# Attention and two expert layers on one core: more of w_in converted ahead of the first unit, its loads ahead of the second batch's, a third buffer of values, block means from half the rows

## The chip, the cores and the metric

The kernel runs on one core of one Trainium2 chip. The metric is the device time of one execution in microseconds (us). TensorE is called PE, VectorE DVE, ScalarE ACT, GpSimd POOL and SyncE SP. SP issues nearly all DMAs, in the order in which they stand in its queue.

## The reference, cut to what matters

Three layers follow each other: a windowed attention with block summaries, a dense layer with a gated activation, and a routed layer of eight experts.

```python
# attention: batch 2, 8 heads, 768 positions, head size 64; blocks of 32, window 16
k_sum = k.reshape(B, H, nb, block, D).max(axis=3)
v_sum = v.reshape(B, H, nb, block, D).mean(axis=3)
scores_l = scale * q @ k^T, masked to |i - j| < window
scores_s = scale * q @ k_sum^T + log(block)
a = softmax(concat(scores_l, scores_s)); out = a @ concat(v, v_sum)
# dense layer on x [1536, 512]: w_in [512, 2048], w_out [2048, 512], stored as float64
h = x @ w_in;  g = h * clip(h + 3, 0, 6) / 6;  y = g @ w_out
# routed layer: every token to one of 8 experts, 192 tokens each
out[mask_e] = relu(y[mask_e] @ w1[e]) @ w2[e]
```

## The kernel before

**Tiles and units.** The 1536 positions are 12 tiles of 128 (n = 0 to 11; six for each batch), and three tiles make a unit (u = 0 to 3). Attention works in halves (n, h) of four heads each. For a half, `front` (L373) multiplies queries with the window of keys on PE (L383) and reduces the scores on DVE (L391); `soften` exponentiates on ACT (L402) and normalises with DVE (L404, L405) and POOL (L406); `turn` transposes the weights on PE (L414), and ACT copies them to a buffer `at` (L416); `values` multiplies with the values on PE (L429). `emit_x` splits a finished tile into a high part on ACT (L447) and a low part on DVE (L78), the form in which the dense layer takes it. `q_prep` transposes the next tile's queries (L353, L355); `window` copies the next tile's keys (L368).

**The weights of the dense layer.** w_in comes as float64 in 16 slices of 512 KB through four buffers `win64` (`w_in_load`, L247). `w_conv` makes float32 of a slice by three DVE instructions (L272), after which the buffer is loaded with the slice four further on; `w_split` makes a high part on ACT (L289) and a low part on POOL (L290).

**The block means of values.** `vsum_load` brings a batch's values with eight rows to a partition (`vs`). The means come of matmuls with a matrix `zones` (`vsum_mul`, L199). For the first batch all eight rows are multiplied and summed by PE; for the second, `vsum` first adds them on POOL (L191) to one row. `vsum_place` copies the means into each of the buffers `VW` that hold values: into the first on DVE (L203), into the second on ACT (L204).

**Order.** There is no scheduler that moves instructions: each engine runs them in the order in which they are recorded. `drive` records several streams against each other: it takes the next piece of the stream that is least far, by hand-given costs and by the shares of the stretch in which each stream is to run. In the first call the streams are `prologue()` (unit 0's attention, total `ATTS[0]`, and the first half of tile 3) and the conversion of the first `AHEAD` slices, which begins at the share `S0`. In the second call they are the dense layer's first matmul for unit 0 (`gemm1`, L621 to L623: 12 matmuls for each of 16 columns f, results in two PSUM banks in turn), attention of unit 1, and the rest of the conversion. For each f, ACT copies the bank (L624) and DVE gates it (L637), which frees the bank for the f after next. The list `soon` holds work such as loads and low parts that is recorded after the next piece. Keys of the second batch are transposed in `kprep` (L334) ahead of tile 6.

Of the kernel before, what the change touches and what calls it, by code (L numbers as in the profile page):

```python
# [43 lines left out]
SEEK, COUNT = 4600, 1900  # L44
ROUTE = 100000
CLAG = 2
AHEAD = 4
EARLY = 13
LEFT = 4
VLAG = 0  # L50
VN = 3
ATTS = [31212, 20565, 23910, 18810]
END = [0.92, 0.92, 0.92]
S0 = 0.27
S1 = 0.7
LX = 4
TAIL = [0, 1], [2]
# [31 lines left out]
def build(ctx, tc, q, k, v, w_in, w_out, w_gate, w1, w2, out):  # L89
# [54 lines left out]
    LAG = 2  # L144
    Abuf = [att.tile([128, 4, KEYS], FT, name=f"A{i}") for i in range(LAG + 1)]
    kw = att.tile([128, HP, 2, KEYS], FT)
    VW = [att.tile([128, 2, H, D], FT, name=f"VW{i}") for i in range(2)]

    def warm(n):

# [13 lines left out]
    def load_rows(kind, src, b, i):  # L164
        if src is k:
            x = k1[i % 4]
        else:
            x = att.tile([128, H, D], FT, name="raw", bufs=3)
        SP.dma_start(x, src[b, :, i * 128:(i + 1) * 128, :].rearrange("h s d -> s h d"))
        raw[kind, b, i] = x  # L170

# [3 lines left out]
    def load_v(n):  # L175

        b, i = divmod(n, 6)
        for g in range(2):
            lo = i * 128 + g * QG - W
            a, z = max(lo, 0), min(lo + WIN, S)  # L180
            SP.dma_start(VW[n % 2][a - lo:z - lo, g], v[b, :, a:z, :].rearrange("h s d -> s h d"))

    RH = [slice(4 * i, 4 * i + 4) for i in range(2)]

# [3 lines left out]
    def vsum(b):  # L188
        m = KR // 2
        while m:  # L190
            POOL.tensor_tensor(vs[:, :, :m], vs[:, :, :m], vs[:, :, m:2 * m], op=OP.add)  # L191
            m //= 2

    means = []

    def vsum_mul(i, last):
        if i == 0:
            means.append(bank(4))
        PE.matmul(means[-1][:KEYS], zones, vs[:, :, i], start=i == 0, stop=last)  # L199

    def vsum_place():
        pv = means[-1][WIN:KEYS, None].rearrange("p a (h d) -> p a h d", d=D).to_broadcast([NB, 2, H, D])
        DVE.tensor_copy(VW[0][WIN:KEYS], pv)  # L203
        ACT.activation(VW[1][WIN:KEYS], pv, AF.Copy)  # L204

    for g in range(2):
        hs = slice(HP * g, HP * g + HP)
# [202 lines left out]
    def turn(n, h):  # L410
        A = Abuf[(2 * n + h) % (LAG + 1)]
        p = bank(2)
        for c in range(4):
            PE.transpose(p[:KEYS, c * 128:(c + 1) * 128], A[:, c], ident)  # L414
        at = att.tile([128, 4, 128], FT, name="at", bufs=3)
        ACT.activation(at[:KEYS], p[:KEYS].rearrange("p (c s) -> p c s", c=4), AF.Copy)  # L416
        ats[n, h] = at

    def values(n, h):
        vw = VW[n % 2]  # L420
        if h == 0:
            xps[n] = bank(4 if n % 2 else 7)
        at = ats.pop((n, h))
        for pr in range(2):
            hp = 2 * h + pr
            for g in range(2):
                at0 = hp * 128 + g * QG
                for s in range(2):
                    PE.matmul(xps[n][64 * s:64 * s + 64, at0:at0 + QG], vw[:KEYS, g, 2 * hp + s, :],  # L429
                              at[:KEYS, 2 * pr + s, g * QG:(g + 1) * QG], start=True, stop=True, skip_group_check=True)  # L430
        if h == 1:
            u, j = divmod(n, UT)
            xlater.append(n)
            if n + 2 < NT:
                soon.append(partial(load_v, n + 2))

    def emit_x():
        while xlater:
# [14 lines left out]
    def halves():  # L453
        for n in range(UT, NT):
            b, i = divmod(n, 6)
            if b and i == 0:
                vsum(b)
                yield from kprep(b)
                q_prep(n)
                window(n)  # L460
                yield 2400
            for h in range(2):
                t = pend.pop(0) if len(pend) >= LAG else None
                if t:
                    turn(*t)
                    turned.append(t)
                    yield 660
                after = h == 1 and i < 5
                first = (n, h) == (UT, 1)
                if not first:  # L470
                    front(n, h, after)
                    yield 1250 + 450 * after
                pend.append((n, h))
                while turned:
                    if turned[0] == (6 * b, 0):
                        vsum_mul(0, True)
                        vsum_place()
                    values(*turned.pop(0))
                    yield 1000
                emit_x()  # L480
                if first:
                    yield 1
                    front(n, h, after)
                    yield 1250 + 450 * after
                yield from soften()
                emit_x()
                if (n, h) == (UT, 0):
                    for g in range(2):
                        vsum_load(1, g)
                    for j in range(4):  # L490
                        load_rows("kraw", k, 1, j)
            if i == 5:
                while pend or turned:
                    if turned:
                        yield 700
                        values(*turned.pop(0))
                        yield 1000
                        emit_x()
                    if pend:
                        yield 800  # L500
                        t = pend.pop(0)
                        turn(*t)
                        turned.append(t)
                        yield 660
# [269 lines left out]
    def prologue():  # L774
        soft = []

        def half(n, h, after=False):
            front(n, h, after)
            soft.append(soften())
            next(soft[-1])  # L780
            pend.append((n, h))
# [14 lines left out]
        yield 600  # L796
        for c in kprep_first(1):
            yield c
        half(0, 0)
        yield 1250  # L800
        qprep_first(1)
        window(0, slice(2, 4))
        yield 600
        half(0, 1, True)
        rest()
        yield 1250
        def block_means(i):
            for j in range(i, i + 2):
                vsum_mul(j, j == KR - 1)

        def both(t):
            values(*t)
            emit_x()
# [1 line left out]
        half(1, 0)  # L815
        rest()
        yield 1250
        block_means(0)
        yield 1700
        turned_one()  # L820
        yield 660
        block_means(2)
        yield 1700
        half(1, 1, True)
        rest()
        yield 1700
        turned_one()
        yield 660
        block_means(4)
        yield 1700  # L830
        half(2, 0)
        rest()
        yield 1250
        block_means(6)
        vsum_place()
        yield 1700
        turned_one()
        yield 660
        for i in range(2):
            both(turned.pop(0))  # L840
            yield 1000
        half(2, 1, True)
        rest()
        yield 1700
        turned_one()
        yield 660
        both(turned.pop(0))
        yield 1000
        rest()
        yield from attend_unit(0)  # L850

    w_in_load(0)
    for g in range(2):
        vsum_load(0, g)
    w_in_load(1)
    load_v(0)
    load_v(1)
    for j in range(2, NW):
        w_in_load(j)
    for n in range(2):  # L860
        load_rows("qraw", q, 0, UT + n)

    def splits():
        for s in range(NF + CLAG):
# [439 lines left out]
```

## Time and profile before

| | us |
|---|---|
| median of 3 runs (587.82 to 588.29) | 587.87 |
| the profiled execution | 584.98 |
| its span | 583.0 |
| PE busy | 548.8 |
| DVE busy | 356.2 |
| ACT busy | 291.7 |
| POOL busy | 163.9 |

The page gives busy time by engine and groups of instructions by source line and shape; the views used below are cut from the same trace. A time in brackets behind a row is how long the engine stood idle before it, and what is taken to have ended that idleness. PEclk is the clock that PE was granted, as a share of 2.4 GHz. A busy time of PE includes the overlap of matmuls that follow each other.

### The profile page before, as it was taken

What the parts mean: (1) busy time and instruction counts of PE and PEld (TensorE: products, weight loads), DVE (VectorE), ACT (ScalarE), POOL (GpSimd) and SP (SyncE); (2) the same over time, 40 slices, a digit from 0 to 9 for tenths busy, and PEclk for the clock granted to TensorE, in tenths of its full rate; (3) what the DMA queues carried; (4) which work ended last, traced back from release to release, by engine and by line L of the source; (5) the groups of instructions that cost most, each with busy time, mean ns of one, the idle gap of its engine ahead of it and who ended that gap; (6) DMA issues with size and microseconds to landing.
All of it is one profiled execution on the core that took longest, in us unless ns stands there. A gap on an engine that the chain in (4) does not pass through costs nothing.

```text
span 583.0 us, 10815 instructions
## 1 busy us (share of the span) xinstructions
PE 548.8 (94%) x3867; PEld 458.5 (79%) x3867; DVE 356.2 (61%) x1022; ACT 291.7 (50%) x698; POOL 163.9 (28%) x197
## 2 busy tenths in 40 slices
PE   6768789989999999999999999999999999999993
PEld 6447678879889989986677777778789888988882
DVE  6577795644543288750045655553588888888880
ACT  4556464456544445561132232234576777677750
POOL 1124348111111032582244444456001100111011
PEclk9789899999999999999999999999999999999998
DMA  9978962302110145430042000004589888998811
GB/s 235 231 193 171 276 177 48 77 20 47 28 36 19 47 141 176 140 105 2 1 126 91 1 1 1 1 18 183 155 262 289 251 242 249 288 254 233 255 47 33
DMA packets 98270, 75.05 MB, mean 129 GB/s; under 512 B 38112, under 2 KB 84704, under 8 KB 98208
## 3 DMA queue, kind: packets, MB, share of 16 engines
q1 hardware_dynamic: 96224, 67.96, 43.2%
q0 software_dynamic: 1984, 6.32, 3.0%
q8 instruction: 33, 0.54, 0.4%
q14 instruction: 29, 0.24, 0.1%
HBM read 67.55 MB, written 6.71 MB: 127 GB/s over the span
## 4 chain that ended last, share of the span: by engine, by line
PE 53%; issue 27%; DVE 8%; DMA 5%; POOL 3%; ACT 2%; SPq 0%; POOLq 0%; DVEq 0%; ACTq 0%
PE bank L738 8%; PE bank L739 7%; PE bank L740 7%; PE bank L621 6%; PE bank L622 5%; PE bank L623 5%; POOL out_dram L1107 3%; DVE bank L272 2%; PE bank L649 2%; PE bank L383 2%; PE bank L199 2%; PE bank L429 2%; PE bank L414 1%; DMA big<-in_moe_w_out_dram 1%; PE bank L309 1%
## 5 line engine op out<-in xcount | busy, mean ns | idle before, releaser
L621 PE MATMUL bank<-x,wh 128*128 128x384 f32 x256 | 91.7, 358 | 4.2 <-DVE t L637 2.1
L299 DVE TENSOR_TENSOR wl<-t,wh 128x1024 fp32r<-128x1024 f32 x64 | 77.0, 1220 | 20.5 <-ACT wh L298 18.1
L623 PE MATMUL bank<-x,wl 128*128 128x384 f32 x256 | 86.7, 339 | 2.5 <-POOL wl L290 2.5
L622 PE MATMUL bank<-x,wh 128*128 128x384 f32 x256 | 86.4, 338 | 0.4 <-DVE x L78 0.3
L715 ACT ACTIVATE thx<-t 128x384 fp32r<-128x384 f32 (+2 forms) x80 | 36.2, 459 | 94.6 <-PE bank L739 94.0
L624 ACT ACTIVATE t<-bank,three 128x384 f32<-128x384 f32 x64 | 37.1, 580 | 89.1 <-PE bank L623 87.1
L738 PE MATMUL bank<-wh,thx 128*128 128x512 f32 x192 | 79.2, 412 | 0.0
L716 POOL TENSOR_TENSOR tlx<-t,thx 128x384 fp32r<-128x384 f32 (+1 forms) x56 | 56.0, 1002 | 77.4 <-ACT thx L715 70.7
L740 PE MATMUL bank<-wh,tlx 128*128 128x512 f32 x192 | 75.3, 392 | 0.1
L739 PE MATMUL bank<-wl,thx 128*128 128x512 f32 x192 | 75.0, 390 | 0.0
L1132 PE MATMUL bank<-x,wh 128*128 128x384 f32 x256 | 73.7, 360 | 0.5 <-DVE x L1058 0.5
L298 ACT ACTIVATE wh<-t 128x1024 fp32r<-128x1024 f32 x64 | 65.6, 1047 | 0.0
L1134 PE MATMUL bank<-x,wl 128*128 128x192 f32 x256 | 64.2, 251 | 0.0
L637 DVE SCALAR_TENSOR_TENSOR t<-t,bank 128x384 f32<-128x384 f32 x64 | 34.9, 549 | 41.1 <-ACT t L624 41.1
L406 POOL TENSOR_TENSOR A<-A,sm 128x480 f32<-128x480 f32 x24 | 23.7, 987 | 128.0 <-ACT at L416 65.8
L1107 POOL DMA_INDIRECT out_dram<-t,idx x16 | 14.9, 931 | 141.5 <-DVE t L1156 136.0
L621 PEld LDWEIGHTS bank<-x,wh 128*128 128x128 f32 x256 | 48.2, 188 | 8.3 <-DVE t L637 3.1
L623 PEld LDWEIGHTS bank<-x,wl 128*128 128x128 f32 x256 | 48.3, 189 | 3.2 <-POOL wl L290 3.2
L622 PEld LDWEIGHTS bank<-x,wh 128*128 128x128 f32 x256 | 48.5, 189 | 1.0 <-DVE x L78 0.9
L1134 PEld LDWEIGHTS bank<-x,wl 128*128 128x128 f32 x256 | 48.9, 191 | 0.3
L1132 PEld LDWEIGHTS bank<-x,wh 128*128 128x128 f32 x256 | 48.1, 188 | 1.2 <-DVE x L1058 0.8
L1148 PE MATMUL bank<-wh,t 128*128 128x512 f32 x128 | 48.9, 391 | 0.0
(194 smaller groups left out, 1014.5 us busy)
## 6 DMA issues: line engine op xcount, KB each, us to landing
t<-in_moe_w_dram SPq DMA_DIRECT2D x128, 256.0 KB, 4.5
t<-in_moe_w_in_dram SPq DMA_DIRECT2D x16, 512.0 KB, 5.7
big<-in_moe_w_out_dram SPq DMA_DIRECT2D x16, 512.0 KB, 3.3
VW<-in_v_dram SPq DMA_DIRECT2D x20, 192.0 KB, 3.7
t<-in_v_dram SPq DMA_DIRECT2D x4, 768.0 KB, 11.8
raw<-in_q_dram SPq DMA_DIRECT2D x9, 256.0 KB, 4.7
t<-xs SPq DMA_DIRECT2D x8, 258.0 KB, 4.4
t<-in_k_dram SPq DMA_DIRECT2D x4, 384.0 KB, 6.0
```

Of the source, the lines that this page charges most:

```text
L298: ACT.activation(hi, x, AF.Copy)
L299: DVE.tensor_tensor(lo, x, hi.bitcast(FT), op=OP.subtract)
L621: PE.matmul(p, wh[:, kk, :], xh[:, kk, :], start=kk == 0, stop=False)
L622: PE.matmul(p, wh[:, kk, :], xl[:, kk, :], start=False, stop=False)
L623: PE.matmul(p, wl[:, kk, :], xh[:, kk, :], start=False, stop=kk == KD - 1)
L716: (DVE if placed[0] else POOL).tensor_tensor(ths[i][1], t, ths[i][0].bitcast(FT), op=OP.subtract)
L738: PE.matmul(acc[j], th[:, c], WH[s], start=f == 0, stop=False)
L739: PE.matmul(acc[j], th[:, c], WL[s], start=False, stop=False)
L740: PE.matmul(acc[j], tl[:, c], WH[s], start=False, stop=f == NF - 1)
L1132: PE.matmul(p, a[:, kk, :], xt[:, kk].rearrange("p c s -> p (c s)"), start=kk == 0, stop=False, skip_group_check=True)
L1134: PE.matmul(p[:, :CAP], b[:, kk, :], xt[:, kk, 0, :], start=False, stop=kk == KD - 1, skip_group_check=True)
L1148: PE.matmul(p, x, w, start=m == 0 and i == 0, stop=m == NM - 1 and i == 2)
```

## The change

Six slices of w_in instead of four are converted in the first call of `drive`, whose total and starting share are changed with it (`AHEAD`, `ATTS[0]`, `S0`). There are three buffers of values instead of two, and the load of tile n + 3 instead of n + 2 follows the values of tile n. Buffers `raw` (queries) and `at` go from three to two. For the first batch, DVE adds the upper four rows of `vs` to the lower four, and PE multiplies four rows instead of eight. The first loads stand in another order, and the second batch's loads of keys and values are recorded in tile 5 instead of tile 3, keys first. In the prologue, the second part of the query preparation stands between the scores and the softmax of the first half, and some pieces stand in another order.

```diff
-AHEAD = 4
+AHEAD = 6
-ATTS = [31212, 20565, 23910, 18810]
+ATTS = [27812, 20565, 23910, 18810]
-S0 = 0.27
+S0 = 0.3
...
-    VW = [att.tile([128, 2, H, D], FT, name=f"VW{i}") for i in range(2)]
+    VW = [att.tile([128, 2, H, D], FT, name=f"VW{i}") for i in range(3)]
...
-            x = att.tile([128, H, D], FT, name="raw", bufs=3)
+            x = att.tile([128, H, D], FT, name="raw", bufs=2)
...
     def vsum(b):
         m = KR // 2
         while m:
-            POOL.tensor_tensor(vs[:, :, :m], vs[:, :, :m], vs[:, :, m:2 * m], op=OP.add)
-            m //= 2
+            (POOL if b else DVE).tensor_tensor(vs[:, :, :m], vs[:, :, :m], vs[:, :, m:2 * m], op=OP.add)
+            m = m // 2 if b else 0
...
-        ACT.activation(VW[1][WIN:KEYS], pv, AF.Copy)
+        for x in VW[1:]:
+            ACT.activation(x[WIN:KEYS], pv, AF.Copy)
...
-        at = att.tile([128, 4, 128], FT, name="at", bufs=3)
+        at = att.tile([128, 4, 128], FT, name="at", bufs=2)
...
-            if n + 2 < NT:
-                soon.append(partial(load_v, n + 2))
+            if n + 3 < NT:
+                soon.append(partial(load_v, n + 3))
...
-                if (n, h) == (UT, 0):
+                if (n, h) == (5, 0):
+                    for j in range(4):
+                        load_rows("kraw", k, 1, j)
                     for g in range(2):
                         vsum_load(1, g)
-                    for j in range(4):
-                        load_rows("kraw", k, 1, j)
...
-        half(0, 0)
-        yield 1250
+        front(0, 0, False)
         qprep_first(1)
+        soft.append(soften())
+        next(soft[-1])
+        pend.append((0, 0))
+        yield 1850
         window(0, slice(2, 4))
-        yield 600
         half(0, 1, True)
...
-                vsum_mul(j, j == KR - 1)
+                vsum_mul(j, j == KR // 2 - 1)
...
         half(1, 0)
         rest()
         yield 1250
-        block_means(0)
-        yield 1700
+        vsum(0)
         turned_one()
...
     for g in range(2):
         vsum_load(0, g)
+    load_v(0)
     w_in_load(1)
-    load_v(0)
+    w_in_load(2)
     load_v(1)
-    for j in range(2, NW):
-        w_in_load(j)
-    for n in range(2):
-        load_rows("qraw", q, 0, UT + n)
+    w_in_load(3)
+    load_rows("qraw", q, 0, UT)
+    load_v(2)
+    load_rows("qraw", q, 0, UT + 1)
```

Lines of the changed kernel below the new ones are numbered one to three higher.

SP's queue around the second batch's loads, before (in_moe_w_in_dram is w_in; VW_94 and VW_95 are the buffers of values, raw is a tile of queries, t<-in_v_dram the values for the block means):

```order
L247 DMA t<-in_moe_w_in_dram 128x4x256 x2
L181 DMA VW_94<-in_v_dram 96x8x64 x2
L169 DMA raw<-in_q_dram 128x8x64
L247 DMA t<-in_moe_w_in_dram 128x4x256
L181 DMA VW_95<-in_v_dram 96x8x64 x2
L173 DMA t<-in_v_dram 96x8x256 x2
L169 DMA t<-in_k_dram 128x8x64 x4
L247 DMA t<-in_moe_w_in_dram 128x4x256
L181 DMA VW_94<-in_v_dram 96x8x64 x2
```

SP's queue around the same loads now:

```order
L248 DMA t<-in_moe_w_in_dram 128x4x256 x3
L169 DMA raw<-in_q_dram 128x8x64
L248 DMA t<-in_moe_w_in_dram 128x4x256
L181 DMA VW_94<-in_v_dram 80x8x64
L181 DMA VW_94<-in_v_dram 96x8x64
L248 DMA t<-in_moe_w_in_dram 128x4x256 x2
L169 DMA t<-in_k_dram 128x8x64 x4
L173 DMA t<-in_v_dram 96x8x256 x2
L181 DMA VW_95<-in_v_dram 96x8x64 x2
```

The batch's loads stood ahead of nine slices of w_in, the first of them right behind; now the last two of w_in stand right ahead of them.

DVE in the prologue, between the scores of half (1, 0) and those of half (1, 1), before (bank_337 is scratch of the conversion):

```order
L404 TENSOR_SCALAR sm<-sm 128x4
L405 RECIPROCAL sm<-sm 128x4
L272 TENSOR_SCALAR bank_337<-t 128x512
L272 SCALAR_TENSOR_TENSOR bank_337<-t,bank_337 128x512
L272 SCALAR_TENSOR_TENSOR t<-t,bank_337 128x512
L391 ISA A_90,sm<-bank_353,mask 128x120
```

DVE at the same place now, with the addition of values (L191) among the conversion:

```order
L405 TENSOR_SCALAR sm<-sm 128x4
L406 RECIPROCAL sm<-sm 128x4
L273 TENSOR_SCALAR bank_341<-t 128x512
L191 TENSOR_TENSOR t<-t 96x8x256
L273 SCALAR_TENSOR_TENSOR bank_341<-t,bank_341 128x512
L392 ISA A_90,sm<-bank_352,mask 128x120
```

The addition came in, and the last step of the conversion moved behind the scores of (1, 1).

## Rows read from the trace of the kernel before

**Rows 1.** Busy time by engine in long stretches; (x) counts instructions:

```profile
core 0: us, PE busy (x) PEld busy (x) DVE busy (x) ACT busy (x) POOL busy (x), PEclk, DMA share, GB/s
0.00:50.00 50.00, 35.45 (x448) 25.92 (x449) 31.58 (x128) 26.29 (x82) 11.51 (x19) 0.86 0.87 206
50.00:93.50 43.50, 37.66 (x315) 32.90 (x313) 38.49 (x105) 25.04 (x73) 20.96 (x19) 0.96 0.87 201
93.50:250.00 156.50, 152.29 (x1231) 138.47 (x1231) 85.75 (x258) 79.76 (x213) 39.95 (x35) 1.00 0.26 72
250.00:583.00 333.00, 323.36 (x1880) 261.20 (x1877) 200.39 (x534) 160.56 (x331) 91.47 (x127) 0.99 0.45 134
```

**Rows 2.** The same view, finer, with the same columns:

```profile
25.30:39.00 13.70, 9.52 (x103) 5.15 (x103) 10.29 (x42) 6.43 (x21) 2.62 (x3) 1.00 0.87 232
39.00:45.80 6.80, 5.94 (x66) 4.81 (x67) 2.36 (x13) 3.72 (x13) 2.54 (x3) 0.50 0.34 92
45.80:50.00 4.20, 2.67 (x56) 2.13 (x53) 2.38 (x6) 3.68 (x12) 1.54 (x2) 1.00 0.78 168
64.30:93.50 29.20, 23.45 (x195) 20.07 (x193) 28.09 (x72) 16.02 (x46) 15.44 (x14) 0.94 0.74 190
69.70:73.10 3.40, 3.40 (x24) 2.96 (x26) 3.26 (x5) 1.25 (x3) 0.74 (x2) 0.50 1.09 310
```

**Rows 3.** Timeline of PE's weight loads: start, us, instruction, [idle before, releaser]:

```profile
66.30 0.19 PEld L621 LDWEIGHTS bank<-x,wh 128*128 128x128 f32 x1 [1.10 <-ACT wh L289]
68.91 0.19 PEld L623 LDWEIGHTS bank<-x,wl 128*128 128x128 f32 x1 [2.31 <-POOL wl L290]
...
93.51 0.19 PEld L621 LDWEIGHTS bank<-x,wh 128*128 128x128 f32 x1 [1.06 <-DVE t L637]
```

**Rows 4.** Timeline of SP's queue and DVE; then loads, with KB, us to landing:

```profile
47.75 10.88 SPq L169 DMA_DIRECT2D t<-in_k_dram  x4
58.72 1.17 SPq L247 DMA_DIRECT2D t<-in_moe_w_in_dram  x1
64.31 0.69 DVE L272 TENSOR_SCALAR bank<-t 128x512 int32<-128x512 int32 x1 [3.21 <-DMA t<-in_moe_w_in_dram]
...
t<-in_v_dram SPq DMA_DIRECT2D x2, 768.0 KB, 9.2
```

**Rows 5.** Stretch, DVE busy (count), clock, DMA share, GB/s of line L272 alone:

```profile
50.00:93.50 43.50, 24.20 (x36) 0.96 0.87 201
```

**Rows 6.** Timeline of PE and DVE in the prologue:

```profile
16.99 0.95 PE L383 MATMUL bank<-kw,t 64*64 64x120 f32 x16 [1.80 <-ACT t L324]
27.89 0.28 DVE L391 CUSTOM_DVE_ANT_0 A<-bank,mask 128x120 f32<-128x120 f32 x1 [3.38 <-PE bank L383]
38.86 0.97 PE L353 MATMUL bank<-ident,raw 128*128 128x128 f32 x4 [2.86 <-issue]
...
43.60 1.08 PE L383 MATMUL bank<-kw,qT 64*64 64x120 f32 x16
49.03 0.64 PE L383 MATMUL bank<-kw,qT 64*64 64x120 f32 x16
50.01 0.42 PE L621 MATMUL bank<-x,wh 128*128 128x384 f32 x1
```

**Rows 7.** Groups by line, 0 to 50 us; L299 of the whole span: busy, mean ns:

```profile
L199 PE MATMUL bank<-t,zones 96*120 96x512 f32 x16 | 9.6, 729 | 0.0
L204 ACT ACTIVATE VW<-bank 24x1024 f32<-24x1024 f32 x1 | 1.0, 1017 | 1.1 <-DVE VW L203 1.1
L213 POOL MEMSET VW<- 128x1024 f32 x2 | 1.8, 941 | 0.0
...
L299 DVE TENSOR_TENSOR wl<-t,wh 128x1024 fp32r<-128x1024 f32 x64 | 77.0, 1220 | 20.5 <-ACT wh L298 18.1 <-DMA t<-in_moe_w_dram 2.4
```

**Rows 8.** Timeline around the second batch's start, POOL and PE:

```profile
96.05 8.43 POOL L191 TENSOR_TENSOR t<-t 96x2048 f32<-96x2048 f32 x3
101.17 0.60 PE L334 MATMUL bank<-ident,t 128*128 128x128 f32 x4
119.75 0.99 POOL L406 TENSOR_TENSOR A<-A,sm 128x480 f32<-128x480 f32 x1 [15.27 <-ACT qT L355]
```

More of the change, by code (lines that the diff above doesn't have):

```diff
@@ L180, in load_v @@
             a, z = max(lo, 0), min(lo + WIN, S)
-            SP.dma_start(VW[n % 2][a - lo:z - lo, g], v[b, :, a:z, :].rearrange("h s d -> s h d"))
+            SP.dma_start(VW[n % 3][a - lo:z - lo, g], v[b, :, a:z, :].rearrange("h s d -> s h d"))
     RH = [slice(4 * i, 4 * i + 4) for i in range(2)]
@@ L419, in values @@
     def values(n, h):
-        vw = VW[n % 2]
+        vw = VW[n % 3]
         if h == 0:
@@ L817, in prologue @@
         yield 1250
-        block_means(0)
-        yield 1700
+        vsum(0)
         turned_one()
         yield 660
-        block_means(2)
-        yield 1700
         half(1, 1, True)
@@ L828, in prologue @@
         yield 660
-        block_means(4)
+        block_means(0)
         yield 1700
@@ L833, in prologue @@
         yield 1250
-        block_means(6)
+        block_means(2)
         vsum_place()
         yield 1700
[L837 to L844, printed above, removed]
+        both(turned.pop(0))
+        yield 1000
         turned_one()
@@ L848, in prologue @@
         yield 1000
+        half(2, 1, True)
+        rest()
+        yield 1700
+        both(turned.pop(0))
+        yield 1000
+        turned_one()
+        yield 660
         rest()
```

## The prediction

> **What bounds the kernel now.** I read the stretches of the trace first [rows 1]. Behind 93.5 us TensorE (PE) is busy 152.29 of 156.5 us and then 323.36 of 333 us: the change touches nothing that costs time there, and PE sets it. The losses lie ahead: in the prologue (0 to 50 us) the granted clock is 0.86 and no engine is full, and in the first 43.5 us of unit 0 PE is busy 37.66 us, but VectorE (DVE) 38.49 us. Next come the finer stretches [rows 2]: from 64.3 to 93.5 us DVE is busy 28.09 of 29.2 us. There DVE is the bound and PE waits for it. Third, the waits of PE's weight loads between 64 and 94 us [rows 3]: six of over 0.5 us, the first at 66.30 (1.10 us), the last at 93.51 (1.06 us, for the gate of DVE), the longest 2.31 us for the low half of a slice of w_in, and all six together 7.1 us. From 69.7 to 73.1 us PE also runs at a granted clock of 0.50, so it does about 1.7 us less work there.
>
> Fourth, what starts the full stretch of DVE: at 64.31 DVE had stood 3.21 us, waiting for a slice of w_in [rows 4]. That slice's load was issued only at 58.72, because the four loads of the second batch's keys had occupied the issue queue of SP for 10.88 us from 47.75. These loads are wanted only at 101.17 us, when PE transposes the keys [rows 8].
>
> **The change, part by part.**
>
> *Unit 0.* Six slices instead of four are converted before its first matmul. The 36 DVE instructions of L272 from 50 to 93.5 us take 24.20 us [rows 5], 0.67 us each; two slices are six of them, 4.0 us. The 3.2 us wait goes too: the SP order puts keys and block-mean loads of batch two behind the last slice of w_in, and the slices that unit 0 wants then wait only for a free buffer, which an earlier conversion frees well ahead (counted from zero, slice seven's buffer comes free when slice three is converted, before unit 0 starts). So DVE needs 38.5 - 4.0 = 34.5 us plus the 43.5 - 38.5 - 3.2 = 1.8 us in which it stood otherwise: 36.3 us. PE alone needs 43.5 - 7.1 - 1.7 = 34.7 us. DVE stays the bound, but by only 1.6 us, so now and then the two will wait for each other in turn: I take 37.3 us, with 36.2 and 38.0 as ends of this case. Gain 6.2 us. Late next is DVE's gate again, and behind the last slice PE.
>
> *Start of unit 0.* Three things move it; before it starts at 50.01 [rows 6]. (a) Query preparation is put ahead of the first softmax: ACT copies the queries before eight softmax instructions instead of after them. The second score matmuls, which stood 1.80 us for that copy and began at 16.99, can begin about 0.9 us earlier, when the key windows are there. (b) The means: eight matmuls (16 rows) cost 9.6 us [rows 7]; four remain, so 4.8 us of PE go. A DVE addition over 96 x 2048 elements comes instead. An addition of 1024 elements takes 1.22 us [rows 7], so this takes between 1.2 us (that row itself) and 2.45 us (twice it); it has twice the elements, so I take 2.4. It cannot start before both halves of the values have landed and stands in DVE's order ahead of the next score reduction. By hand, that reduction moves from 27.89 [rows 6] to about 25.5: PE's scores are ready near 22.9, and the addition eats half of what the absent matmuls give. (c) Two more slices, 4.0 us, go between DVE's reductions, most behind the second and third query tile. From 25.5 I walk DVE's new order: window copies and a normalisation 2.8 us, four conversions 2.7, the reduction of (2,0) at 30.4; copy of the means at 31.6 to 32.9, when values can start on PE. ACT now copies the means twice, 1.02 us each [rows 7], so the third tile copy and, behind it, the first output come about a microsecond later than the copy of the means alone would ask: the query transposes that began at 38.86 [rows 6] begin at 37.5. From there ACT is the chain (softmax, tile copy, tile copy, softmax, output), as before, and reaches the first matmul of unit 0 at 48.6, a lead of 1.4 us.
>
> That walk has all matmuls at the full clock. The trace grants 0.50 from 39.0 to 45.8 [rows 2], after PE was busy 9.52 of 13.7 us with holes. At half clock scores take 1.08 us instead of 0.64 [rows 6]. The new order has less PE work in this stretch, so I expect the low level at least as long. About eight bursts of 0.4 us more come, half of them behind an ACT that is late anyway: 1.6 us. Ends: 1.4 us earlier and 1.0 us later (all eight on the path and a slow first 1 us of unit 0); I take 0.2 us earlier.
>
> The Trainium skill speaks against this part of the change: "TensorE: Matmul & The Clock Gate", section "What's actually happening", says that the throttled clock is the default and activity releases it, so taking matmuls out of a thin stretch can cost clock. The trace agrees so far that low stretches follow thin ones. By that rule the start would be the late end, and the sum 1.2 us worse.
>
> *At no cost.* The third memset of a value buffer (0.94 us [rows 7]) lies on POOL while PE waits for the first keys; constants behind it reach DVE about 0.9 us later, against a first use that stands at least as long behind PE. Two tile buffers and two query buffers instead of three: each tile copy now waits for the values two tiles before it, which PE has already done in either order; a query load waits for transposes two tiles before, and SP's queue holds slices of w_in behind it, which are not wanted for some 10 us. If that cover went, it would cost DVE the 3.2 us again.
>
> *Second batch.* Its loads go out when slice eleven frees its buffer, by the walk near 72 us, where they were issued at 47.75 [rows 4]. The four loads of keys, 10.88 us of issue, are in by about 84 us, and the values, which took 9.2 us to land [rows 4], by about 93. PE wants the keys at 101.17 less 6.4, near 95. POOL's addition of values takes 8.43 us [rows 8]: it began at 96.05 and would now run from 93 to 101.5, ahead of a normalisation that came at 119.75 after 15.27 us of idleness and now comes near 113. Cover is some 11 us for each. No cost.
>
> **Sum.** The profiled execution took 584.98 us, its span 583.0; the median of the other runs is 587.87, 2.9 us more. Against the profile: 584.98 - 6.2 - 0.2 = 578.6. The parts move a stretch by the same microseconds in either kind of run, so against the median: 587.87 - 6.4 = **581.5 us**. The ends of this case: 36.2 with the early start gives 579.2, 38.0 with the late start 583.4.
>
> **Rivals.** (1) *The prologue is DVE's.* If the 6.4 us that DVE gains there (4.0 + 2.4) all lie on the path and only the 4.8 us of matmuls leave it, unit 0 starts 1.6 us late, and 1 to 3 us of low clock come on top; with 6.2 us gained later that gives 583.4 to 586.7. For it: each reduction now stands behind conversions. Against: DVE is busy only 31.58 of the first 50 us [rows 1], and ACT is the chain at the end. (2) *PE becomes the bound of unit 0*: 34.7 us, and the start 1.4 us early: 587.87 - 8.8 - 1.4 = 577.7. For it: DVE's margin is 1.6 us. Against: the two engines wait for each other through two banks. (3) *The clock, and slower than before.* If PE stays at the low level from 25.3 us into unit 0, some 5.5 us of matmuls (9.52 less the means) and the 2.67 us of [rows 2] double, and the first 7 us of unit 0 lose 3.4: 11.6 us, against a gain of 7.6 without it, gives 591.9. It decides from 7.6 us of added matmul time on the path. Against: clock came back at 45.8 although the stretch ahead of it had only two thirds of its time filled. (4) *It doesn't do what it says*: the slices' loads still come late, since a load needs its buffer and SP waits in order behind query loads that now wait for a buffer; DVE still stands 3.2 us, and what it is spared in unit 0 (4.0 us) it pays in the prologue: 586.7 to 589. Against: buffers come free before 48 us by the walk.
>
> **Chances.** Forecast 0.53, rival 1 0.20, rival 2 0.13, rival 3 0.06, rival 4 0.08. A measurement of this kernel can tell about 0.2% (1.2 us) from no change. Faster 0.53 + 0.20 + 0.13 = 0.86, same 0.08, slower 0.06. The range 578.0 to 586.7 leaves out rivals 3 and 4 and the lower half of rival 2, 0.2 together.
>
> **What would show it.** In the new profile the first matmul of unit 0 starts between 48.6 and 51 us; DVE has no wait of over 1 us for w_in there; PE's waits for DVE and POOL in unit 0 fall from 7.1 to 2 or 3 us; the step that ended at 93.5 ends near 87; the stretches behind it keep their lengths to 1 us; keys land before PE asks for them. Wrong would be: a start behind 52 us, granted clock 0.50 inside unit 0 for more than 3.4 us, DVE waiting for the values ahead of the addition, or PE waiting for the second batch's keys.

## The result, and the profile after

The changed kernel takes 582.81 us (median of 4 runs, 581.76 to 583.78) where the kernel before takes 587.85 us beside it (4 runs, 587.59 to 588.29). The ratio is 0.9913, with an interval of 0.9894 to 0.9933: 5.0 us faster, between 3.9 and 6.2 us. The prediction said 6.4 us. Its sum has two terms, and the trace of after shows them apart: the gain in unit 0 came nearly as worked out, and the start of unit 0, forecast 0.2 us earlier, came 2.4 us later.

The stretches of after, cut where those of [rows 1] are cut (first matmul of unit 0; the wait of PE for DVE's gate that stands last in [rows 3]; the end of unit 3). The columns are start:end, length, busy time of PE, PE's weight loads, DVE, ACT and POOL (instructions in brackets), granted clock, share and rate of DMA:

```profile
0.00:52.40 52.40, 39.64 (x440) 28.64 (x441) 40.07 (x138) 28.11 (x85) 15.68 (x22) 0.69 0.96 218
52.40:90.10 37.70, 36.00 (x315) 32.31 (x313) 33.73 (x96) 24.31 (x72) 17.94 (x16) 0.98 0.87 194
90.10:246.60 156.50, 152.40 (x1231) 138.56 (x1232) 85.36 (x257) 80.34 (x214) 39.92 (x35) 1.00 0.27 74
246.60:580.00 333.40, 323.50 (x1879) 260.98 (x1877) 200.88 (x534) 160.61 (x331) 91.45 (x127) 0.99 0.45 134
...
19.50:53.70 34.20, 28.36 (x224) 18.23 (x221) 27.23 (x89) 17.88 (x57) 11.86 (x11) 0.50 0.95 208
```

The second row took 43.5 us before and takes 37.7. The third is as long as before to 0.1 us and the fourth to 0.4. The first is 2.4 us longer, with a clock of 0.69 where it had 0.86. The last row says why: from 19.5 to 53.7 us PE was at a granted clock of 0.50, the lower of its two levels, without a break, 1.2 us of it inside unit 0. Before, the same level stood from 18.5 to 25.3 and from 39.0 to 45.8.

A finer ruler for unit 0 is the first output of its first and of its thirteenth column, the ACT instruction that reads PE's result. First before, then after (start, us, instruction, [idle before, releaser]):

```profile
52.75 0.58 ACT L624 ACTIVATE t<-bank,three 128x384 f32<-128x384 f32 x1 [1.80 <-DMA t<-in_v_dram]
95.92 0.58 ACT L624 ACTIVATE t<-bank,three 128x384 f32<-128x384 f32 x1 [0.73 <-PE bank L623]
```

```profile
55.39 0.58 ACT L625 ACTIVATE t<-bank,three 128x384 f32<-128x384 f32 x1 [1.96 <-PE bank L624]
92.50 0.58 ACT L625 ACTIVATE t<-bank,three 128x384 f32<-128x384 f32 x1 [1.80 <-PE bank L624]
```

From first to thirteenth is 43.17 us before and 37.11 after: 6.06 us less. The experiments below are read by this distance. (The lines of after lie one lower: L272 is now L273.)

What DVE waited for from 50 to 95 us in after (us in total, times, longest), and its conversions in unit 0 alone (busy, count):

```profile
DVE t L638 <- ACT t L625: 4.3, 4, 1.8
DVE sm L405 <- ACT A L403: 1.0, 1, 1.0
DVE x L78 <- ACT x L448: 0.7, 1, 0.7
```

```profile
52.40:90.10 37.70, 20.60 (x30) 0.98 0.87 194
```

No wait for a slice of w_in is left, against the 3.21 us of [rows 4], and 30 instructions of 20.60 us stand where 36 of 24.20 us stood [rows 5]. What DVE waits for now is ACT, which waits for PE. PE's weight loads still wait in four places, where [rows 3] sums six to 7.1 us:

```profile
71.39 0.19 PEld L622 LDWEIGHTS bank<-x,wh 128*128 128x128 f32 x1 [0.34 <-DVE t L638]
73.94 0.55 PEld L430 LDWEIGHTS bank<-at,VW 120*64 120x64 f32 x16 [0.50 <-ACT at L417]
...
78.12 0.19 PEld L622 LDWEIGHTS bank<-x,wh 128*128 128x128 f32 x1 [0.99 <-DVE t L638]
...
90.08 0.19 PEld L622 LDWEIGHTS bank<-x,wh 128*128 128x128 f32 x1 [0.81 <-DVE t L638]
```

That is 2.6 us, three of the four for DVE's gate. But PE is now the fuller of the two, 36.00 against DVE's 33.73 of 37.70 us, and the chain of work that ended last changes sides (start, us, engine and line; each row is the last or the first of its stretch):

```profile
67.19 0.19 PE bank L624
67.44 0.15 DVE A L392
...
78.12 0.44 PE bank L622
...
83.39 0.58 ACT t L625
...
90.08 0.45 PE bank L622
```

It lies on PE up to 67.4 and from 78.1 to 83.4, some 21 us in all, on DVE for some 14 us, and on ACT and POOL for most of the rest. Neither engine alone bounds unit 0 any more.

The prologue is read in the chain of work that ended last (start, us, engine and line):

```profile
22.22 2.70 DVE t L191
24.95 3.77 PE bank L199 x4
28.72 1.01 PE bank L384 x16
29.73 3.71 PE bank L199 x4
33.47 1.24 DVE VW L203
...
39.40 1.13 PE bank L354 x4
...
43.80 1.08 PE bank L415 x4
44.88 1.01 PE bank L384 x16
...
51.75 1.04 PE bank L354 x4
```

The addition (L191) and both pairs of mean matmuls (L199) lie on it. Eight rows of the means take 7.5 us at the low clock, where sixteen took 9.6 us before [rows 7]. Halving them has brought PE 2.1 us, not 4.8. Each burst of scores or transposes behind them takes 1.0 to 1.1 us, where [rows 6] has 0.64 at the full clock.

The second batch, on SP, POOL and PE, for [rows 4, 8]:

```profile
77.25 4.30 SPq L169 DMA_DIRECT2D t<-in_k_dram  x4
81.59 2.00 SPq L173 DMA_DIRECT2D t<-in_v_dram  x2
```

```profile
93.66 8.45 POOL L191 TENSOR_TENSOR t<-t 96x2048 f32<-96x2048 f32 x3 [1.18 <-PE bank L415]
...
116.32 0.99 POOL L407 TENSOR_TENSOR A<-A,sm 128x480 f32<-128x480 f32 x1 [14.22 <-ACT qT L356]
```

```profile
97.75 0.60 PE L335 MATMUL bank<-ident,t 128*128 128x128 f32 x4
```

The keys' loads, issued 29.5 us later than before, take 4.30 us of SP instead of 10.88, and PE's first transposes of them (97.75) wait for nothing. POOL's addition starts at 93.66, where the prediction had 93, and the next normalisation behind it had stood 14.22 us for something else. That this move costs nothing was right.

One thing does not fit to the microsecond. The two profiled executions are 3.2 us apart (584.98 and 581.76 us), the medians 5.0. The profiled execution of before was 2.9 us under its median, that of after 1.1 us. The start of unit 0 moves between executions: the kernel with only the loads moved, whose prologue is that of before, started it at 50.72, not 50.01, and the run with two value buffers, whose prologue is that of after but for a memset, a copy of the means and a load, at 51.39, not 52.45. So the start is a term of some 1 to 2.4 us, and single traces don't settle it closer.

### The profile page after: what moved, and what is told of

Read it like the earlier page. It is cut to its first block, busy times and chain, and to the rows that moved or that the text cites. A ratio compares the mean times of both kernels' runs of the same rounds, so it can differ in the third digit from the quotient of the medians.

```text
span 580.0 us, 10816 instructions
## 1 busy us (share of the span) xinstructions
PE 551.5 (95%) x3859; PEld 460.5 (79%) x3859; DVE 360.0 (62%) x1023; ACT 293.4 (51%) x700; POOL 165.0 (28%) x198
## 4 chain that ended last, share of the span: by engine, by line
PE 54%; issue 27%; DVE 6%; POOL 5%; DMA 3%; ACT 3%; SPq 0%; POOLq 0%; DVEq 0%; ACTq 0%
PE bank L739 7%; PE bank L622 7%; PE bank L741 6%; PE bank L740 6%; PE bank L624 6%; PE bank L623 6%; POOL out_dram L1110 3%; PE bank L430 2%; POOL xs L672 2%; PE bank L384 2%; PE bank L650 2%; ACT A L403 2%; PE bank L199 1%; PE bank L415 1%; PE bank L310 1%
## 5 line engine op out<-in xcount | busy, mean ns | idle before, releaser
L299 ACT ACTIVATE wh<-t 128x1024 fp32r<-128x1024 f32 x64 | 65.6, 1048 | 0.0
L1137 PEld LDWEIGHTS bank<-x,wl 128*128 128x128 f32 x256 | 48.9, 191 | 0.3
L1151 PE MATMUL bank<-wh,t 128*128 128x512 f32 x128 | 48.9, 391 | 0.0
```

The costliest lines, as they stand in the source:

```text
L299: ACT.activation(hi, x, AF.Copy)
L1137: PE.matmul(p[:, :CAP], b[:, kk, :], xt[:, kk, 0, :], start=False, stop=kk == KD - 1, skip_group_check=True)
L1151: PE.matmul(p, x, w, start=m == 0 and i == 0, stop=m == NM - 1 and i == 2)
```

## Experiments

All ratios are against the kernel before, run beside each kernel. *Lead* is the time from the first score matmul to the first matmul of unit 0 (this leaves out how early the scores could start, which moves by 1.7 us between executions), *unit 0* the distance from the first to the thirteenth column as above, *low clock* the stretches at 0.50 between 15 and 95 us. The last three columns come from the one profiled execution of each kernel.

| kernel | median | ratio, interval | lead | unit 0 | low clock |
|---|---|---|---|---|---|
| before | | | 36.92 | 43.17 | 18.5–25.3, 39.0–45.8, 69.7–73.1 |
| after | 582.81 | 0.9913, 0.9894–0.9933 | 38.89 | 37.11 | 19.5–53.7 |
| means8 | 581.48 | 0.9914, 0.9886–0.9943 | 36.92 | 37.10 | 21.2–28.1, 45.1–52.0 |
| warm | 580.77 | 0.9906, 0.9873–0.9940 | 36.26 | 37.10 | none |
| loads_back | 586.80 | 0.9990, 0.9961–1.0018 | 37.65 | 42.02 | 21.6–48.9, 72.8–79.6 |
| ahead4 | 584.11 | 0.9938, 0.9908–0.9969 | 38.60 | 40.29 | 18.9–53.1 |
| loads_only | 584.16 | 0.9960, 0.9935–0.9985 | 36.91 | 40.32 | 19.7–26.5, 40.2–47.0 |
| ahead_only | 582.29 | 0.9910, 0.9874–0.9945 | 37.66 | 37.24 | 20.2–27.1, 37.3–47.5 |
| values2 | 582.33 | 0.9923, 0.9896–0.9950 | 37.66 | 37.11 | 20.1–47.4 |
| ahead_loads | 582.10 | 0.9914, 0.9892–0.9935 | 37.94 | 37.10 | 21.7–28.5, 38.8–49.0 |
| means8_warm | 579.21 | 0.9859, 0.9832–0.9886 | 36.70 | 37.10 | 38.3–41.7 |
| ahead_warm | 580.86 | 0.9886, 0.9863–0.9909 | 38.71 | 37.11 | 37.4–44.2 |

The theory was that unit 0 gains what DVE is spared there, and that the start is late because of the clock. The rival was that the prologue is DVE's: the addition and the two further conversions lie on its path.

### The eight mean matmuls back

```diff
-            for j in range(i, i + 2):
-                vsum_mul(j, j == KR // 2 - 1)
+            for j in range(2 * i, 2 * i + 4):
+                vsum_mul(j, j == KR - 1)
...
-        vsum(0)
```

> The changed kernel, but the first batch's block means come of all eight rows again: no DVE addition (2.77 us in the trace of the changed kernel), eight matmuls instead of four, four at each of the two places. Theory A (the start of unit 0 came late, at 52.45 us, because PE ran at a granted clock of 0.50 from 19.5 to 53.7 us, and it fell and stayed low since the matmuls of the means left): with them back the clock is at 1.00 for at least part of 25 to 50 us, unit 0 starts between 50.5 and 52.5, and the time is 581.5 to 583.5. Rival B (the matmuls themselves are on the path, whatever the clock): four more at 0.9 us each put the start 2 to 4 us later, 585 to 587.

The ratio is that of after, 0.9914 against 0.9913. Its lead, and the score reduction that stands behind the addition in after (at 25.42 there), as windows of all engines (columns as in the first fence) and as a row of DVE:

```profile
14.52:51.44 36.92, 27.25 (x298) 17.61 (x297) 27.89 (x111) 22.06 (x75) 11.90 (x11) 0.82 1.10 224
```

```profile
23.82 0.27 DVE L392 CUSTOM_DVE_ANT_0 A<-bank,mask 128x120 f32<-128x120 f32 x1
```

The lead is 1.97 us shorter than in after, the reduction comes 1.6 us earlier, and the granted clock, back at 1.00 from 28.1, stayed there up to 45.1. The four kernels with halved means and no extra matmuls (after, loads_back, ahead4, values2) have the low clock for 27.3 to 34.2 us without a break; this one has it twice for 6.9 us. So halving the means, worth 4.8 us of PE in the prediction, bought nothing here that the times can tell: in the trace, what it saves on PE it gives back as an addition on DVE and as clock. This run alone does not tell the clock from DVE's work, since it changes both.

### After, with the clock held up

Sixty extra matmuls of the identity into a bank that nobody reads, in nine places (three are shown), by the kernel's own helper `warm`; nothing else is touched. The trace counts each as two instructions.

```diff
         qprep_first(1)
+        warm(5)
...
         half(0, 1, True)
+        warm(8)
...
         half(1, 0)
+        warm(5)
```

> The changed kernel with 60 extra matmuls of the identity (128 x 128, float32) into a bank that nobody reads, in the holes of PE between 15 and 46 us; nothing else is changed, the outputs are the same. Theory A (the clock sets the late start of unit 0): the granted clock stays at 1.00 for most of 20 to 50 us, unit 0 starts at 49 to 50.5 instead of 52.45, and the time is 580 to 581.5. Rival B (the conversions and the addition on DVE set the start): the clock rises, but unit 0 still starts at 52 or later, 582.5 to 584.

The lead row of this kernel, and that of after (columns as above):

```profile
14.79:51.05 36.26, 32.14 (x411) 26.62 (x409) 29.67 (x107) 22.30 (x75) 11.30 (x11) 1.00 1.01 218
```

```profile
13.56:52.45 38.89, 30.67 (x291) 19.75 (x289) 30.77 (x112) 22.07 (x75) 11.95 (x11) 0.58 0.96 211
```

With 120 more instructions on PE and nearly the same work on DVE (29.67 against 30.77 us) the lead is 2.63 us shorter. That is the clock, and it speaks against the rival: DVE's addition and conversions are all still there. The start itself, 51.05, lies between the two expectations, because the first scores came late (14.79 against 13.56). The other kernels with this prologue fall in line: 38.89 and 38.60 us of lead with 34.2 us of low clock, 37.65 and 37.66 with 27.3, 36.26 with none. The prediction's walk at the full clock put unit 0's start 35.5 us behind the first scores (48.6 less 13.09); 36.26 came out. The gain is shown in the traces only: the median falls by 2.0 us, but the ratio to the runs beside it by 0.0007, or 0.4 us, and its interval contains that of after.

### The second batch's loads back, and six conversions ahead kept

```diff
-                if (n, h) == (5, 0):
-                    for j in range(4):
-                        load_rows("kraw", k, 1, j)
+                if (n, h) == (UT, 0):
                     for g in range(2):
                         vsum_load(1, g)
+                    for j in range(4):
+                        load_rows("kraw", k, 1, j)
```

> The changed kernel, but the second batch's loads of values and keys are recorded in tile 3 again, as before, ahead of most of w_in's slices. Theory A (3.2 of the 6.2 us that unit 0 gained are the DVE's wait for a slice of w_in): DVE stands 2 to 4 us for w_in in unit 0 again, and the time is 585 to 586.5. Rival C (two slices more in hand cover the queue's delay): no such wait, 582.3 to 583.3.

0.9990: with this one part undone, nothing is left that the times can tell. DVE and SP of this kernel:

```profile
71.87 0.70 DVE L273 TENSOR_SCALAR bank<-t 128x512 int32<-128x512 int32 x1 [5.95 <-DMA t<-in_moe_w_in_dram]
```

```profile
52.85 10.75 SPq L169 DMA_DIRECT2D t<-in_k_dram  x4
63.69 1.68 SPq L181 DMA_DIRECT2D VW<-in_v_dram  x2
65.47 1.10 SPq L248 DMA_DIRECT2D t<-in_moe_w_in_dram  x1
```

The slice behind the keys in SP's queue is issued at 65.47, and DVE, ready for it at 65.92, stands 5.95 us, more than the 2 to 4 us expected. Before, DVE was ready at 61.10 for a slice issued at 58.72: here the keys went out 5.1 us later, and DVE came to its slice only 4.8 us later, 0.45 us behind the issue instead of 2.4.

### Four conversions ahead, with the rest of the change

```diff
-AHEAD = 6
+AHEAD = 4
```

> The changed kernel with four slices converted ahead of unit 0 instead of six. Theory A (DVE bounds unit 0 and 4.0 us of its work were moved ahead into its holes): unit 0's stretch from the first to the thirteenth column grows from 37.1 us by 2.5 to 4, while its start gains at most 1 us; the time is 584.5 to 586. Rival D (with the loads out of the way DVE is no bound any more): the stretch keeps its length to 1 us, 582 to 583.

0.9938, and unit 0 takes 40.29 us (54.94 to 95.23):

```profile
54.94 0.58 ACT L625 ACTIVATE t<-bank,three 128x384 f32<-128x384 f32 x1 [1.84 <-PE bank L624]
95.23 0.58 ACT L625 ACTIVATE t<-bank,three 128x384 f32<-128x384 f32 x1 [0.73 <-PE bank L624]
```

So the six DVE instructions are worth 40.29 - 37.11 = 3.2 us there, where the prediction's term was 4.0. The run also bears on the late start. Its lead row (columns as above):

```profile
13.51:52.11 38.60, 31.16 (x290) 20.10 (x289) 26.45 (x106) 21.25 (x73) 9.35 (x9) 0.57 0.94 202
```

DVE has 4.3 us less to do in the lead than in after (26.45 against 30.77), the clock is as low (0.57 against 0.58), and the lead is only 0.3 us shorter. With the extra matmuls it was the other way round: DVE as busy, the clock up, 2.6 us gained. So by these traces it is the clock that makes the start late, and not the conversions on DVE.

### The loads moved, alone

```diff
-                if (n, h) == (UT, 0):
-                    for g in range(2):
-                        vsum_load(1, g)
+                if (n, h) == (5, 0):
                     for j in range(4):
                         load_rows("kraw", k, 1, j)
+                    for g in range(2):
+                        vsum_load(1, g)
```

> The kernel before with one part of the change: the second batch's loads of keys and values are recorded in tile 5, behind w_in's, keys first. Theory A (DVE's 3.2 us wait for w_in goes, and it has nothing else to stand for): the wait at 64.3 us is gone, unit 0 starts at 50 as before, its stretch from the first to the thirteenth column falls from 43.2 to about 40 us, and the time is 584 to 585. Rival C (the queue's delay is hidden elsewhere, DVE just meets the next bound): the stretch falls by less than 1.5 us, 586.5 to 587.5.

0.9960. Unit 0 takes 40.32 us, as in the run before this one, which has the same loads and the same four slices. Its stretch to DVE's gate (columns as above):

```profile
50.70:91.40 40.70, 36.18 (x316) 31.65 (x314) 38.69 (x105) 25.06 (x73) 21.04 (x19) 1.00 0.76 185
```

DVE does the same work as in [rows 1] (38.69 against 38.49 us), in 2.8 us less. The 3.2 us wait is gone, and so is the low clock that stood behind it before (69.7 to 73.1), so the two are not told apart. DVE is busy 38.69 of 40.7 us: the bound, as predicted.

### Six conversions ahead, alone

```diff
-AHEAD = 4
+AHEAD = 6
-ATTS = [31212, 20565, 23910, 18810]
+ATTS = [27812, 20565, 23910, 18810]
-S0 = 0.27
+S0 = 0.3
```

> The kernel before with one part of the change: six slices are converted ahead of unit 0, with the change's totals and shares for the recording; loads stand as before. Theory A: DVE runs ahead but comes to the slice whose load stands behind the second batch's loads, and stands there for 4 to 6 us instead of 3.2; the stretch of unit 0 falls by less than 1.5 us, and the prologue loses up to 1 us; the time is 586.5 to 588. Rival D (conversion ahead is worth its 4.0 us alone): the stretch falls by 3 to 4 us, 583.5 to 585.

The theory fell here. It expected the wait for a slice to come back, as in the run with the loads back; instead three lines of numbers gave the whole gain, 0.9910. Unit 0 takes 37.24 us, from its first to its thirteenth column:

```profile
54.42 0.58 ACT L624 ACTIVATE t<-bank,three 128x384 f32<-128x384 f32 x1 [1.81 <-PE bank L623]
91.66 0.58 ACT L624 ACTIVATE t<-bank,three 128x384 f32<-128x384 f32 x1 [1.79 <-PE bank L623]
```

SP's queue of this kernel:

```profile
42.98 3.21 SPq L247 DMA_DIRECT2D t<-in_moe_w_in_dram  x2
...
50.72 10.92 SPq L169 DMA_DIRECT2D t<-in_k_dram  x4
61.73 1.92 SPq L181 DMA_DIRECT2D VW<-in_v_dram  x2
63.71 0.73 SPq L169 DMA_DIRECT2D raw<-in_q_dram  x1
64.53 2.67 SPq L247 DMA_DIRECT2D t<-in_moe_w_in_dram  x3
```

A slice's load is issued where an earlier slice is converted. Converting earlier puts loads of w_in earlier into the queue: ten of them stand ahead of the keys here, seven before. The keys still hold SP for 10.92 us, with the next slice behind them at 64.53, but by then DVE has ten slices and does not wait for w_in at all. In the run with the loads back, the rest of the change leaves only nine ahead of the keys, and the tenth costs 5.95 us; which part of it does so was not tried. So the wait has two remedies, and which slice stands behind the keys decides.

### Both, alone

The kernel before with the edits of the two runs above and nothing else.

> The kernel before with both roads and nothing else: six slices converted ahead of unit 0, and the second batch's loads put behind the loads of w_in. Theory A (each road removes the same loss, the wait of VectorE for a slice in unit 0, so they do not add up): 0.989 to 0.993, first matmul to gate twelve 37.1 to 37.4 us, as in the run with the conversions alone (0.991, 37.24). Theory B (the two losses are different ones, 0.996 times 0.991): 0.986 to 0.988, and the stretch 36 us or less.

0.9914, and unit 0 takes 37.10 us: the two remedies don't add up. They remove the same wait, and only the conversions remove DVE work as well.

### Two buffers for values

```diff
-    VW = [att.tile([128, 2, H, D], FT, name=f"VW{i}") for i in range(3)]
+    VW = [att.tile([128, 2, H, D], FT, name=f"VW{i}") for i in range(2)]
```

(and each use of three as two)

> The changed kernel with two buffers of values again (a load follows the values of two tiles before; one memset and one copy of the means on ACT less). Theory A (the third buffer changes nothing that the prologue or unit 0 waits for): the time stays at 582 to 583.5, no wait of PE for values of over 0.5 us. Rival E (the third buffer's ACT copy of 1.02 us and memset are on the path): 0.5 to 1 us faster, unit 0 starts before 52 us. Rival F (values come too late with two): PE waits for values of tile 2 and the time is over 584.

0.9923 with an interval that holds the ratio of after. The third buffer is worth nothing that these runs can tell. Unit 0 started at 51.39, which rival E took as its sign, but the low clock also ended 6.3 us sooner than in after, so this does not speak for E alone.

### The eight means and a held clock

After with the eight matmuls and without the addition, and 34 extra matmuls in five places.

> The changed kernel with all eight rows of the block means on PE, no addition on DVE, and 34 extra matmuls of the identity in the holes of PE that this leaves before unit 0; a version that may beat both. Theory A (the clock sets the start): granted clock 1.00 from 20 to 50 us, unit 0 starts 35.5 to 36.7 us behind the first score matmul (38.9 in the changed kernel), and the time is 579.5 to 581.2. Rival B (matmuls of the means are on the path once the clock is up): 37 us or more behind it, 581 to 582.5.

0.9859, 579.21 us: the fastest of all, faster than before by 8.0 us and than after by some 3 us (the intervals do not meet). The low clock is left only from 38.3 to 41.7, and the lead is 36.70 us. Of these 3 us, 2.2 show in the trace as a shorter lead (38.89 to 36.70); the rest is not told apart from the spread of single executions. Against the eight means alone, the kernel that it differs from by nothing but the extra matmuls, the lead is only 0.22 us shorter (36.92 to 36.70) and the intervals touch (0.9886), so what the extra matmuls bring in this kernel stays open.

### The held clock, on the kernel before

The three lines of the run with six conversions ahead, and 34 extra matmuls in the corresponding five places.

> The kernel before with six slices converted ahead, and 34 extra matmuls of the identity into a spare bank in the prologue, for the clock alone; the loads of the second batch, the values' buffers, the order of the prologue and the eight mean matmuls stay as before. Theory A (what the change adds beside the conversions brings nothing, and low clock in the prologue is the only other loss): the first matmul of unit 0 36.3 to 37.0 us behind the first score matmul (37.66 without the extra ones), ratio 0.985 to 0.989. Theory B (the new order of the prologue is needed to use the clock): ratio 0.990 or more, and the distance 37.4 us or more.

Neither theory got all of it: the ratio, 0.9886, is what theory A expected (0.985 to 0.989), but the lead, 38.71 us, is what theory B did, 1.05 us longer than without the extra matmuls. PE of this kernel shows where:

```profile
40.10 3.62 PE L153 MATMUL bank<-ident 128*128 128x128 f32 x16
43.51 0.94 PE L414 MATMUL bank<-ident,A 128*120 128x128 f32 x4
```

In this order eight of the extra matmuls follow the query transposes directly, at a time when the clock was low. They take 3.62 us, and the transposes that ACT and the third tile wait for stand behind them; without them these began at 40.76. The mean clock of the lead is higher than without them (0.91 against 0.77), and the lead is longer all the same. The profiled execution was the slowest of six (583.18 us), so its lead may be a poor picture of the median's. Whether the new order of the prologue is worth something by itself stays open: the interval overlaps those of the run with six conversions alone and of after.

## Why the prediction was right, and where it was not

**Unit 0: the gain right, the bound only in part.** Predicted 43.5 to 37.3 us, ends 36.2 and 38.0; measured 37.7 in the same stretch, 6.06 us by the finer ruler against a gain of 6.2. Its two terms can be read apart: the wait, with the low clock behind it, is worth 2.85 us (43.17 to 40.32, the loads alone; 3.2 predicted), the six DVE instructions 3.2 us (40.29 to 37.11; 4.0 predicted). Both are less than their face, and the 1 us that the prediction had added for DVE and PE waiting for each other covers it. Left over are 2.6 us of PE's waits for DVE and ACT; "2 or 3" was said. What "DVE stays the bound, but by only 1.6 us" says did not come: PE is busy 36.00 us there and DVE 33.73. The 34.7 us for PE took off the 7.1 us for which its weight loads waited, but PE itself stood only 43.5 - 37.66 = 5.8 us; with 1.7 off for the clock that leaves 36.0, and 36.00 came. So rival 2 named half of the mechanism with too low a price, and that 37.3 came so near to 37.7 is in part luck: the sum was DVE's 36.3 and 1 us, the trace has PE's 36.0 and 1.7.

**The start of unit 0: wrong.** Predicted 0.2 us earlier with 1.0 us later as the end, and "a start behind 52 us" as the sign of a wrong step (the step that was to end near 87 ended at 90.1 with it); it came at 52.45, 2.44 us later than before, of which 0.47 lie ahead of the first scores, where the clock rose to its upper level at 9.3 us instead of 8.3. The step that failed is the size of the low clock: "eight bursts of 0.4 us more, half of them behind an ACT that is late anyway: 1.6 us". The prediction took the low stretch of 39.0 to 45.8, 6.8 us, and made it "at least as long"; it stood 34.2 us without a break, from 19.5 on, so the mean matmuls themselves ran in it. Halving them saved 2.1 us instead of 4.8, which is 2.7 us on the chain that the bursts did not contain, and the addition took 2.77 us instead of 2.4. The chain carries this through: the query transposes came at 39.40 instead of 37.5. The run with extra matmuls shows the clock as the cause (2.63 us of lead), and that the walk itself was good to 0.8 us. What rival 1 argued, a prologue bound by DVE, is not what happened, though the lateness it gave (1.6 us and clock on top) looks like it: 4.3 us less of DVE's work shortened the lead by 0.3 us only (four conversions ahead). (Rival 1's own terms add up to 584.3 to 586.3, not to 583.4 to 586.7.)

The Trainium skill, "TensorE: Matmul & The Clock Gate", section "What's actually happening", has the low clock as the default that activity releases. The traces agree in part: 0.50 for 34.2 us with the mean matmuls halved, two stretches of 6.9 us with all eight, and 1.00 from 11.5 us through the rest of the prologue when matmuls of no use were added; but the 28.36 us for which PE was busy in those 34.2 did not release it. The prediction weighed this as the late end of the start, and the start came behind that end.

**The rest: right but for the addition.** "Between 1.2 and 2.45, I take 2.4" was 2.77 in after, above its upper end, and 2.49 with four slices ahead; the score reduction behind it came at 25.42 (25.5 predicted). Memsets, tile and query buffers and the second batch's loads cost nothing that the trace shows: the stretches behind unit 0's gate kept their length within 0.4 us, and PE did not wait for the keys. Rival 3, the clock and slower than before, had the mechanism that did come, but of the 7.6 us that it needed on the path some 2.4 came. Rival 4, slices still late, is what the run with the loads back shows (0.9990, DVE standing 5.95 us); in the change itself the order of SP's queue keeps it away.

**What the prediction took for the cause of the gain** was the loads' new place together with the conversions, and it named them as two separate 3 to 4 us. It did not see that converting ahead moves w_in's loads in SP's queue as well, and so removes the wait alone. Of the whole change three lines carry the gain (0.9910 against 0.9913); buffers, halved means and the new order of the prologue add nothing that these runs can tell.

By the traces the sum is -6.06 + 2.44 = -3.6 us; by the medians it is -5.0, with an interval that begins at -3.9. The difference of some 1.4 us is not shown to come from any one place. The profiled execution of before, 2.9 us under its median, has the earliest first scores (13.09) of all the traces and the shortest stretch behind unit 3. That the median ended only 1.3 us from the forecast is in part luck: the traces' own sum would have put it 2.8 us above.

## What to carry to other kernels

When an engine waits for a load, look at what stands ahead of that load in its issuing queue, and count which load is the first one behind the blocker: moving the blocker back and moving the loads ahead are the same remedy, and need not be paid twice. Taking matmuls out of a stretch where PE is not full can cost as much clock as it saves work (here 2.1 us were saved of 4.8); cost the remaining matmuls there at the lower level too, as the late end, before a gain is counted. Extra matmuls that hold the clock should lie in gaps: sixty of them, in nine places, shortened the lead by 2.6 us, but in another kernel eight of them stood 3.6 us in front of the chain. A wait of PE's weight loads is not idle time of PE; what PE needs alone is read from its own busy time.

## What the hardware showed unexpectedly

The granted clock stayed at 0.50 for 34.2 us although PE was busy 28.36 us of them; at the low level the same work fills more of the time (a burst of scores 1.08 us against 0.64), so a full row of PE's busy time there was no sign that the clock would come back. When the clock first rose differed between executions, at 8.3 to 11.5 us, and the first score matmul moved with it, from 13.09 to 14.79 us. Behind unit 3, where none of these kernels differ, single executions took 334.7 to 336.9 us from ACT's last column to the end of the span, a spread as large as the terms disputed here.

In all five traces that have it, DVE's addition starts while POOL normalises, and ends 2.14 to 2.16 us after POOL's instruction does. In after the two are

```profile
21.77 0.99 POOL L407 TENSOR_TENSOR A<-A,sm 128x480 f32<-128x480 f32 x1 [1.37 <-DVE sm L406]
22.13 2.77 DVE L191 TENSOR_TENSOR t<-t 96x2048 f32<-96x2048 f32 x1
```

Where it started 0.63 us before POOL was done it took 2.77 or 2.78 us, where 0.35 us (four slices ahead) 2.49. It looks as if the addition stood until POOL had finished; no run moves POOL's instruction away, so this is not shown.
